# A table of 187 numbers that moves tasks in the priorities of a list schedule

## The chip, the cores and the metric

One core of one Trainium2 chip. The core has five instruction queues: PE (TensorE, matrix products), DVE (VectorE), ACT (ScalarE), POOL (GpSimd) and SP (SyncE, which here only starts DMA transfers). Each runs its own instructions in the order in which they were written, and waits on semaphores for the others. The metric is the device time of one execution, in microseconds.

## The reference

```
# q, k, v: 8 x 8 x 576 x 64, phi: 8 x 8 x 576 x 32 (batch, heads, tokens, ...)
a = softmax(phi, axis=2)                           # over the 576 tokens
k_m = einsum('bhsm,bhsd->bhmd', a, k)              # 32 memories per head
v_m = einsum('bhsm,bhsd->bhmd', a, v)
attn = softmax(q @ k_m.T / sqrt(64), axis=-1)
x = (attn @ v_m), heads side by side               # 4608 x 512
h = x @ w_in                                       # w_in: 512 x 2048
out = maximum(h, 0)**2 @ w_out                     # w_out: 2048 x 512
```

The two weights come as 64-bit floats.

## The kernel before

**The numerics.** Products run on PE in `fp32r`, and an operand that has to be more exact is kept as a high and a low part, so that a product becomes three matmuls (high by high, high by low, low by high). `decode` turns each 512 KB piece of 64-bit weights into such a pair with a chain of DVE and ACT instructions (L417 to L437, and L450 for the last subtraction). Where the weight goes into `wo`, the low part of the later pieces is added by a DMA that POOL issues (L454).

**The work.** A batch of 576 tokens is one step, and its heads are handled in two halves (`u` is batch and half, as `5_0`). `memory` loads `phi`, `k` and `v`, takes the maximum over the tokens (L516 on DVE, then two transposes on PE, L518 and L521), and forms `k_m` and `v_m` (L540, into the PSUM tile `pkv`). `vw_step` and its relatives multiply `v_m` into `w_in`, so that attention times that product (`vw`) gives `h` without forming `x` (tiles `pvw`, `vw`). `scores`, `first_attention` and `attention` give the softmax `S`, its transpose (`pat`, `at`) and the pair `ath`, `atl`. `mm1` forms `h` (L923), and `r`, `gh`, `glo` are its relu, its square and the low part of the square. `mm2` adds the product with `wo` into `acc` (L953, L954, L956). From the 96th of these steps `fast` does the same with seven products in place of eight for each pair of 256-wide pieces (its `H`, `M` tiles, L1086 and L1115).

**Buffers.** A buffer name stands for a slot that is used again and again, and whoever writes next waits for all that used it before. Two are of interest. The slot `mx` holds both the maximum of L516 and, for batches 5 to 7, the transposed memories `kT`, which POOL stores to DRAM at L601 (`kT_kept`):

```
        mx = st([P, P], F32, "mx", f"mx{u}")
        kT = st([P, 2, 1, M], F32, f"kT{b % 2}{hh}" if b <= QUAD else "mx", f"kT{u}")
```

The weights `wi` that SyncE loads again for the later batches (L461) rotate through three slots, each of which comes free when PE has used the piece in it (L670).

**The order.** None of this is issued as it is written. Each operation is first recorded by `Plan.op`, with the engines that may run it and a cost on each (`ways`), and with what it depends on. `Plan.order` then makes list schedules. Each operation gets a key from how late it may be, `forward` plays the five engines and the wire with these costs and always takes, on an engine that is free, the ready operation of the smallest key, and several rounds with other keys (`backward`) are tried. The keys of the best round are played once more, and the operations are written in the order of the start times that this gives. Where an operation may run on two engines, the play also settles which one.

## Time and profile before

| | |
|---|---|
| median of 3 runs | 770.11 us (768.22 to 772.91) |
| the profiled execution | 768.92 us |
| its span, first to last instruction | 767.2 us |
| mean granted TensorE clock | 0.994 of full speed |
| PE busy | 740.4 us, 97% of the span |
| DVE, ACT, POOL busy | 605.3, 411.1, 75.9 us (79%, 54%, 10%) |

The profiled execution is 1.7 us longer than its span; that part lies before the first and after the last instruction. PE's busy time counts overlapping matmuls once. What PE waits for is read from the list of its waits, and where it waits from the instructions in order of time.

### The profile page before, as it was taken

The numbers are of one execution on the slowest core, as the hardware profiler recorded it, in microseconds if no ns is written. First come the engines' busy times: TensorE is split into PE (matmuls) and PEld (weight loads), VectorE is DVE, ScalarE is ACT, GpSimd is POOL, SyncE is SP. The second block draws the span as 40 slices with busy tenths as digits, with TensorE's granted clock in tenths as the row PEclk, the third lists the DMA queues.
The fourth block names the chain that finished last, engine by engine and source line by source line (L and its number), as shares of the span: only waits on it lengthen the run. The fifth ranks groups of instructions, "written<-read, shape, count | busy, mean of one in ns | idle before, by whom it ended". The sixth has DMA issues, their size and how long they took to land.

```text
span 767.2 us, 14774 instructions
## 1 busy us (share of the span) xinstructions
PE 740.4 (97%) x5374; PEld 649.5 (85%) x5374; DVE 605.3 (79%) x1405; ACT 411.1 (54%) x933; POOL 75.9 (10%) x133
## 2 busy tenths in 40 slices
PE   5988999999999999999999999999999999999997
PEld 3767898888888887888888788888888899999997
DVE  4899999997669798776659445579999868996875
ACT  2666788775653554534345234345565735666642
POOL 4101211110100000001010221111000100000000
PEclk9989999999999999999999999999999999999999
DMA  8987987478755946554385877875410345445421
GB/s 266 321 283 193 290 243 240 166 209 237 210 137 147 275 117 175 176 164 116 102 299 168 276 216 260 269 230 114 109 37 1 73 121 156 138 114 174 129 82 42
DMA packets 82632, 135.62 MB, mean 177 GB/s; under 512 B 26080, under 2 KB 52704, under 8 KB 82560
## 3 DMA queue, kind: packets, MB, share of 16 engines
q1 hardware_dynamic: 67168, 98.40, 44.2%
q0 software_dynamic: 15296, 36.15, 15.7%
q8 instruction: 43, 0.70, 0.4%
q14 instruction: 29, 0.24, 0.1%
q10 hardware_dynamic: 96, 0.13, 0.1%
HBM read 96.14 MB, written 34.80 MB: 171 GB/s over the span
## 4 chain that ended last, share of the span: by engine, by line
PE 44%; issue 33%; DVE 9%; DMA 7%; POOL 4%; ACT 1%; SPq 1%; POOLq 0%; DVEq 0%; ACTq 0%
PE h L1058 7%; PE h L923 6%; PE acc L956 4%; PE acc L953 4%; PE acc L954 4%; POOL vw_kept L709 2%; DMA out_dram<-o 2%; PE accl L1169 2%; DMA wo<-work 2%; PE pkv L540 2%; PE accl L1184 1%; DMA raw<-in_moe_w_out_dram 1%; PE pvw L670 1%; PE psc L753 1%; PE Mb L1115 1%
## 5 line engine op out<-in xcount | busy, mean ns | idle before, releaser
L923 PE MATMUL h<-ath,vw 128*128 128x320 f32 (+1 forms) x768 | 159.2, 301 | 1.4 <-ACT ath L846 0.9
L953 PE MATMUL acc<-wo,gh 128*128 128x512 f32 x384 | 156.6, 408 | 0.4 <-ACT gh L929 0.4
L954 PE MATMUL acc<-wo,gh 128*128 128x512 f32 x384 | 151.1, 393 | 1.4 <-DMA wo<-work 1.4
L923 PEld LDWEIGHTS h<-ath,vw 128*128 128x128 f32 x768 | 127.0, 190 | 12.4 <-ACT r L927 1.6
L956 PE MATMUL acc<-wo,glo 128*128 128x512 f32 x384 | 117.3, 402 | 0.8 <-DVE glo L933 0.7
L927 ACT ACTIVATE r<-h 128x256 f32<-128x256 f32 (+1 forms) x142 | 57.1, 408 | 61.8 <-PE h L923 56.3
L929 ACT ACTIVATE gh<-r 128x512 fp32r<-128x512 f32 x96 | 60.7, 632 | 47.9 <-DVE r L928 39.1
L953 PEld LDWEIGHTS acc<-wo,gh 128*128 128x128 f32 x384 | 72.3, 188 | 15.6 <-ACT gh L929 0.9
L954 PEld LDWEIGHTS acc<-wo,gh 128*128 128x128 f32 x384 | 72.4, 188 | 14.3 <-DMA wo<-work 1.7
L923 PE MATMUL h<-atl,vw 128*128 128x320 f32 (+1 forms) x384 | 82.9, 297 | 0.5 <-DVE atl L847 0.5
L956 PEld LDWEIGHTS acc<-wo,glo 128*128 128x128 f32 x384 | 68.9, 189 | 13.8 <-DVE glo L933 1.4
L933 DVE TENSOR_TENSOR glo<-r,gh 128x512 fp32r<-128x512 f32 x96 | 65.3, 681 | 5.5 <-ACT r L931 4.6
L923 PEld LDWEIGHTS h<-atl,vw 128*128 128x128 f32 x384 | 62.2, 190 | 0.8 <-DVE atl L847 0.8
L1058 PE MATMUL h<-ath,vw 128*128 128x256 f32 (+1 forms) x256 | 52.3, 296 | 0.0
L345 ACT CAST vw<-pvw 64x512 fp32r<-64x512 f32 (+1 forms) x64 | 37.1, 580 | 22.7 <-PE pvw L670 19.5
L931 ACT ACTIVATE r<-r 128x576 f32<-128x576 f32 x68 | 46.6, 685 | 1.6
L928 DVE TENSOR_SCALAR r<-h 128x320 f32<-128x320 f32 (+1 forms) x50 | 22.8, 457 | 25.5 <-PE h L923 25.1
L1058 PEld LDWEIGHTS h<-ath,vw 128*128 128x128 f32 x256 | 39.9, 188 | 0.5 <-issue 0.2
L678 DVE TENSOR_TENSOR vw<-pvw,vw 64x512 fp32r<-64x512 f32 x48 | 33.0, 686 | 2.0 <-ACT vw L345 1.0
L932 DVE TENSOR_TENSOR r<-r 128x576 f32<-128x576 f32 x28 | 21.2, 757 | 15.6 <-ACT gl L930 13.6
L709 POOL DMA_DIRECT2D vw_kept<-fold x32 | 17.3, 540 | 111.3 <-DVE fold L706 91.5
L753 PE MATMUL psc<-qT,kb 128*128 128x256 f32 (+1 forms) x96 | 27.5, 408 | 0.2 <-DVE S L757 0.2
(251 smaller groups left out, 1615.1 us busy)
## 6 DMA issues: line engine op xcount, KB each, us to landing
vw<-vw_kept SPq DMA_DIRECT2D x192, 128.0 KB, 3.1
wi<-w_in_kept SPq DMA_DIRECT2D x40, 512.0 KB, 5.0
vw_kept<-fold POOLq DMA_DIRECT2D x32, 512.0 KB, 4.2
KV<-in_k_dram SPq DMA_DIRECT2D x16, 512.0 KB, 4.3
KV<-in_v_dram SPq DMA_DIRECT2D x16, 512.0 KB, 5.5
raw<-in_moe_w_out_dram SPq DMA_DIRECT2D x16, 512.0 KB
raw<-in_moe_w_in_dram SPq DMA_DIRECT2D x16, 512.0 KB, 4.8
w_in_kept<-wi POOLq DMA_DIRECT2D x16, 512.0 KB, 5.2
```

The source lines that it names most:

```text
L345: nc.scalar.copy(o, i) if e == "ACT" else ENG[e].tensor_copy(o, i)
L678: vec({"DVE": 700}, lambda e, part=part, pr=pr: nc.vector.tensor_sub(part(1), pw()[pr], part(0).bitcast(F32)), [pw, (V, (0, hf))], [(V, (1 ...
L753: nc.tensor.matmul(pq()[:, 0:32 * n], kb()[:, x].rearrange("p h m -> p (h m)"), qT()[:, x, 0:n].rearrange("p c t -> p (c t)"), start=(x == ...
L923: nc.tensor.matmul(p()[:, 0:n], V()[:, l, hh, c0:c0 + P], x()[:, hh, cs], start=(i == 0), stop=(i == 5))
L927: op({"ACT": act(n) - 40, **({} if b < 2 else {"DVE": tt(n)})}, lambda e, cs=cs, n=n, p=p: nc.scalar.activation(r()[:, cs], p()[:, 0:n], A ...
L929: op({"ACT": act(SM)}, lambda e: nc.scalar.activation(gh(), r()[:, 0:SM], AF.Square), [r], [gh])
L931: op({"ACT": act(S), **({} if b < 2 or b == FAST - 1 else {"DVE": tt(S)})}, lambda e: nc.scalar.activation(r(), r(), AF.Square) if e == "A ...
L933: vec({"DVE": tt(SM)}, lambda e: nc.vector.tensor_sub(glo(), r()[:, 0:SM], gh().bitcast(F32)), [r, gh], [glo])
L953: nc.tensor.matmul(a(), gh()[:, c], t()[:, 0], start=f0, stop=False)
L954: nc.tensor.matmul(a(), gh()[:, c], t()[:, 1], start=False, stop=False)
L956: nc.tensor.matmul(a(), glo()[:, c], t()[:, 0], start=False, stop=f1)
L1058: nc.tensor.matmul(p()[:, at:at + n], V()[:, l, hh, f0:f0 + P], x()[:, hh, cs], start=(i == 0), stop=(i == 5))
```

## The change

Each call of a function that is marked `plan.named` begins a new task, each call's end another, and so does every twelfth operation within one; tasks are numbered in the order of recording, up to about 1000. `MOVED` gives 187 of them a number. After the best keys are found, each operation of task n has its key changed by 100 times `MOVED[n]`, in the unit of the keys (ns), and the last play of `forward` uses these keys. Nothing else differs: operations, buffers, transfers and their sizes are the same. Since the new text stands above the rest, a line n of the kernel before is some 20 to 60 lines further down in the changed one (L518 has become L562, L923 L975, L953 L1006).

```
+PART = 12
+MOVED = {
+    10: 23, 11: 291, 12: 70, 16: 47, 18: 49, 22: -30, 26: -2, 30: -23, 32: 201, 34: 36, 36: 18, 40: 85, 42: 47,
...
+    979: -46, 989: -18, 990: 35, 995: 320,}
...
+    def begin(self):
+
+        self.tasks += 1
+        self.task, self.steps = self.tasks, 0
+
+    def named(self, fn):
+
+        def run(*args, **more):
+            self.begin()
+            got = fn(*args, **more)
+            self.begin()
+            return got
+
+        return run
...
+        if self.steps == PART:
+            self.begin()
+        self.steps += 1
...
+        o.task = self.task
...
-        self.forward(best[1])
+        moved = [k + 100 * MOVED.get(o.task, 0) for k, o in zip(best[1], self.ops)]
+        self.forward(moved)
...
+    @plan.named
     def decode(kind, j, h, room):
...
+    @plan.named
     def memory(b, hh, where=None):
```

The same mark stands on `wi_again`, `vw_alone`, `vw_step`, `vw_quad`, `vw_again`, `scores`, `first_attention`, `attention`, `mm1`, `mm2`, `combine`, `fast` and `fast_left`.

**What moves in the start-up.** PE's queue around the second transposes of the first attention (`pat0_1`, from the softmax `S0_1`), before:

```order
L540 MATMUL pkv1_0_495<-KV1_0_273,phi1_0_215 32x64 x40
L843 MATMUL pat0_1_591<-ident_63,S0_1_436 128x128 x4
L850 MATMUL patl0_599<-ident_63,S0_1_436 128x128
L923 MATMUL h0_0_614<-ath0_474,vw0_0_0_454 128x256 x2
L923 MATMUL h0_0_614<-atl0_536,vw0_0_0_454 128x256 x2
L923 MATMUL h0_0_614<-ath0_474,vw0_0_0_454 128x256 x2
L651 MATMUL pvw0_1_0_626<-wi0_1_0_597,VTh00_89 128x256 x4
L651 MATMUL pvw0_1_0_626<-wi0_1_0_597,VTl00_95 128x256 x2
L576 MATMUL pkt1_0_636<-ident_63,kvx1_0_623 128x128
L923 MATMUL h0_1_640<-ath0_474,vw0_0_0_454 128x320 x2
```

and after:

```order
L584 MATMUL pkv1_0_496<-KV1_0_278,phi1_0_215 32x64 x40
L620 MATMUL pkt1_0_603<-ident_63,kvx1_0_589 128x128
L620 MATMUL pvt1_0_610<-ident_63,kvx1_0_589 128x128
L893 MATMUL pat0_1_615<-ident_63,S0_1_431 128x128 x4
L900 MATMUL patl0_622<-ident_63,S0_1_431 128x128
L696 MATMUL pvw0_1_0_624<-wi0_1_0_596,VTh00_89 128x256 x4
L696 MATMUL pvw0_1_0_624<-wi0_1_0_596,VTl00_95 128x256 x2
L696 MATMUL pvw0_1_0_624<-wi0_1_1_559,VTh00_89 128x256 x4
L696 MATMUL pvw0_1_0_624<-wi0_1_1_559,VTl00_95 128x256 x2
L562 MATMUL pmx1_1_645<-ident_63,mx1_1_599 128x128
L975 MATMUL h0_0_648<-ath0_474,vw0_0_0_472 128x256 x2
```

The transposes `pkt1_0` and `pvt1_0` of batch 1's memories and the twelve `pvw0_1_0` matmuls, which stood behind the first group of `h`, now stand ahead of it, and so does `pmx1_1`.

DVE's queue at the same place, up to the last multiplication of that softmax (L867), before:

```order
L865 TENSOR_SCALAR rz0_1_526<-rz0_1_526 128x20
L847 TENSOR_TENSOR atl0_536<-pat0_0_464,ath0_474 128x512
L421 TENSOR_SCALAR work_518<-work_518 128x512
L866 RECIPROCAL rz0_1_526<-rz0_1_526 128x20
L435 SCALAR_TENSOR_TENSOR work_518<-raw_380,work_518 128x512
L867 TENSOR_TENSOR S0_1_436<-S0_1_436,rz0_1_526 128x640
L437 TENSOR_TENSOR work_518<-work_518 128x512
L437 TENSOR_TENSOR work_423<-work_423 128x512
```

and after (the multiplication is L917):

```order
L479 TENSOR_TENSOR work_436<-work_436 128x512
L463 TENSOR_SCALAR work_519<-work_519 128x512
L914 TENSOR_REDUCE rz0_1_581<-S0_1_431 128x20
L477 SCALAR_TENSOR_TENSOR work_519<-raw_380,work_519 128x512
L622 SCALAR_TENSOR_TENSOR kvx1_0_589<-pkv1_0_496,rs1_0_526,par_76 128x128
L479 TENSOR_TENSOR work_519<-work_519 128x512
L915 TENSOR_SCALAR rz0_1_581<-rz0_1_581 128x20
L621 TENSOR_SCALAR kvx1_0_589<-pkv1_0_496,rs1_0_526 128x128
L916 RECIPROCAL rz0_1_581<-rz0_1_581 128x20
L560 TENSOR_REDUCE mx1_1_599<-phi1_1_309 128x128
L917 TENSOR_TENSOR S0_1_431<-S0_1_431,rz0_1_581 128x640
```

Five instructions, the two L437 of `decode`, two for `kvx1_0` and the maximum `mx1_1`, and the small reciprocal of `rs1_0`, have passed from behind it to ahead of it.

**What moves near 284 us.** PE's queue, with the product `pvw1_4_0` that frees a slot of `wi`, and `pkv5_0`, the memories of half 5_0, before:

```order
L555 MATMUL pkv5_0_3440<-ones_70,asum5_0_3420 128x1
L953 MATMUL acc2_0_1_3187<-wo20_935,gh36_3411 128x512
L954 MATMUL acc2_0_1_3187<-wo20_935,gh36_3411 128x512
L670 MATMUL pvw1_4_0_3449<-wi1_4_0_3250,VTh10_2284 128x256 x2
L670 MATMUL pvw1_4_0_3449<-wi1_4_0_3250,VTl10_2298 128x256
L670 MATMUL pvw1_4_0_3449<-wi1_4_0_3250,VTh10_2284 128x256 x2
L670 MATMUL pvw1_4_0_3449<-wi1_4_0_3250,VTl10_2298 128x256
L540 MATMUL pkv5_0_3440<-KV5_0_3131,phi5_0_2990 32x128 x20
```

and after, the product, and then `pkv5_0` with its neighbours (18 rows lie between the two):

```order
L716 MATMUL pvw1_4_0_3443<-wi1_4_0_3216,VTh10_2296 128x256 x2
L716 MATMUL pvw1_4_0_3443<-wi1_4_0_3216,VTl10_2304 128x256
L716 MATMUL pvw1_4_0_3443<-wi1_4_0_3216,VTh10_2296 128x256 x2
L716 MATMUL pvw1_4_0_3443<-wi1_4_0_3216,VTl10_2304 128x256
L975 MATMUL h38_1_3454<-ath2_2836,vw1_0_3_3308 128x320 x2
L975 MATMUL h38_1_3454<-atl2_2845,vw1_0_3_3308 128x320 x2
```

```order
L1006 MATMUL acc2_0_0_3123<-wo21_959,gh37_3485 128x512
L1007 MATMUL acc2_0_0_3123<-wo21_959,gh37_3485 128x512
L584 MATMUL pkv5_0_3494<-KV5_0_3179,phi5_0_3007 32x128 x20
L1009 MATMUL acc2_0_1_3186<-wo20_954,glo36_3388 128x512
L1006 MATMUL acc2_0_1_3186<-wo21_959,gh37_3485 128x512
```

The product has moved from right ahead of `pkv5_0` to well ahead of it; the maximum `pmx5_1`, 32 rows behind `pkv5_0` in both, is still that far behind. The slot of `wi` that the product frees is the one for `wi1_5_1`, which SyncE loads next.

**What moves near 605 us.** ACT's queue at the first step of `fast`, with the two casts of `H96`, before:

```order
L345 COPY o5_2_6974<-acc5_0_2_6212 128x512
L1076 ACTIVATE XD_6960<-XD_6960 128x256
L345 COPY o5_1_6985<-acc5_0_1_6204 128x512
L1002 CAST wo71_2070<-E7_1_6902 128x256
L345 COPY o5_3_6999<-acc5_0_3_6219 128x512
L1086 CAST H96_7002<-X96_6950 128x512
L1086 CAST H96_7002<-XD_6960 128x384
```

and after:

```order
L1117 ACTIVATE XD_6952<-h96_0_6927 128x256
L1131 ACTIVATE XD_6952<-XD_6952 128x256
L386 COPY o5_0_6975<-acc5_0_0_6187 128x512
L1056 CAST wo71_2094<-E7_1_6925 128x256
L1141 CAST H96_6991<-X96_6942 128x512
L386 COPY o5_3_7002<-acc5_0_3_6255 128x512
L1117 ACTIVATE X97_7008<-h97_0_6979 128x256
L1141 CAST H96_6991<-XD_6952 128x384
```

Of the four copies `o5_x`, three stood ahead of the casts here and one was on DVE; now one stands ahead of them, one between them, and two are on DVE. On PE, the six matmuls of `h97_0` that stood behind the first products `Mb96` now stand ahead of them.

## Rows read from the trace of the kernel before

**Rows 1.** The page: the span, the busy time of each engine, and the chain of work that ended last by engine.

```profile
span 767.2 us, 14774 instructions
...
PE 740.4 (97%) x5374; PEld 649.5 (85%) x5374; DVE 605.3 (79%) x1405; ACT 411.1 (54%) x933; POOL 75.9 (10%) x133
...
PE 44%; issue 33%; DVE 9%; DMA 7%; POOL 4%; ACT 1%; SPq 1%; POOLq 0%; DVEq 0%; ACTq 0%
```

**Rows 2.** Busy time by stretch of the span, whole program. Columns: stretch and its length, busy us (instructions) of PE, PEld, DVE, ACT and POOL, the granted TensorE clock as a share of full speed, the share of DMA, GB/s.

```profile
44.60:51.50 6.90, 5.55 (x23) 5.20 (x23) 6.02 (x14) 3.50 (x10) 1.06 (x2) 0.51 1.06 329
...
60.00:200.00 140.00, 137.37 (x981) 118.88 (x980) 129.01 (x270) 104.17 (x226) 23.32 (x33) 1.00 0.77 226
200.00:760.00 560.00, 556.66 (x3849) 494.11 (x3848) 430.37 (x1033) 276.77 (x645) 39.36 (x72) 1.00 0.53 154
```

**Rows 3.** Waits of PE: the instruction and what it waited for, us in total, times, longest.

```profile
PE pat L843 <- DVE S L867: 1.7, 1, 1.7
...
PE pmx L518 <- DVE mx L516: 1.5, 1, 1.5
...
PE acc L954 <- DMA wo<-work: 1.4, 1, 1.4
PE Mb L1115 <- ACT H L1086: 1.1, 1, 1.1
```

**Rows 4.** PE between 40 and 60 us in order of time. Columns: start us, us, engine, line, operation, out<-in, shape, count, [idle before it <- what ended that].

```profile
43.77 0.66 PE L843 MATMUL pat<-ident,S 128*128 128x128 f32 x4 [1.71 <-DVE S L867]
...
45.51 0.58 PE L923 MATMUL h<-ath,vw 128*128 128x256 f32 x1 [0.85 <-ACT ath L846]
...
46.81 0.58 PE L923 MATMUL h<-atl,vw 128*128 128x256 f32 x1 [0.50 <-DVE atl L847]
...
58.90 0.30 PE L518 MATMUL pmx<-ident,mx 128*128 128x128 f32 x1 [1.59 <-DVE VTl L629]
59.41 0.73 PE L956 MATMUL acc<-wo,glo 128*128 128x512 f32 x2 [0.21 <-DVE glo L933]
```

**Rows 5.** DVE in the same stretch, the same columns.

```profile
43.64 1.29 DVE L437 TENSOR_TENSOR work<-work 128x512 f32<-128x512 f32 x2
44.84 0.15 DVE L569 RECIPROCAL rs<-rs 128x1 f32<-128x1 f32 x1
44.91 1.24 DVE L516 TENSOR_REDUCE mx<-phi 128x128 f32<-128x640 f32 x1
...
47.47 0.34 DVE L578 SCALAR_TENSOR_TENSOR kvx<-pkv,rs,par 128x128 f32<-128x128 f32 x1
47.73 0.34 DVE L577 TENSOR_SCALAR kvx<-pkv,rs 128x128 f32<-128x128 f32 x1
```

**Rows 6.** The second half of `wo20` on DVE and POOL, then its use on PE, the same columns.

```profile
73.12 0.68 DVE L450 TENSOR_TENSOR wo<-work,wo 128x512 fp32r<-128x512 f32 x1
...
74.10 0.88 POOL L454 DMA_DIRECT2D wo<-work  x1 [1.58 <-DVE wo L450]
...
81.24 0.50 PE L953 MATMUL acc<-wo,gh 128*128 128x512 f32 x1 [0.39 <-ACT gh L929]
83.13 0.50 PE L954 MATMUL acc<-wo,gh 128*128 128x512 f32 x1 [1.38 <-DMA wo<-work]
```

**Rows 7.** The DMAs that POOL issues at L454 between 70 and 90 us, from issue to landing.

```profile
DMA to landing us min/median/max: 5.2/8.7/9.0
```

**Rows 8.** The store of `kT5_0` near 287 us. First SyncE's queue and POOL, then the time to landing of this store and of the three stores after it, then DVE and PE; columns as in rows 4.

```profile
284.31 0.32 SPq L461 DMA_DIRECT2D wi<-w_in_kept  x1
285.71 0.38 SPq L470 DMA_DIRECT2D KV<-in_k_dram  x1
...
301.48 0.32 SPq L461 DMA_DIRECT2D wi<-w_in_kept  x1
304.49 0.38 SPq L470 DMA_DIRECT2D KV<-in_k_dram  x1
...
287.14 0.57 POOL L601 DMA_DIRECT2D kT_kept<-kT  x1 [1.20 <-DVE vx L604]
...
DMA to landing us min/median/max: 6.3/6.3/6.3
...
DMA to landing us min/median/max: 3.6/3.7/3.9
...
293.48 1.25 DVE L516 TENSOR_REDUCE mx<-phi 128x128 f32<-128x640 f32 x1 [1.46 <-DMA kT_kept<-kT]
...
284.00 0.28 PE L670 MATMUL pvw<-wi,VTl 128*128 128x256 f32 x1
...
294.88 0.30 PE L518 MATMUL pmx<-ident,mx 128*128 128x128 f32 x1 [1.47 <-DVE mx L516]
```

**Rows 9.** The start of the last stage near 605 us: ACT, then PE, the same columns.

```profile
605.65 0.41 ACT L1002 CAST wo<-E 128x256 fp32r<-128x256 f32 x1
605.96 0.59 ACT L345 COPY o<-acc 128x512 f32<-128x512 f32 x1
606.44 0.63 ACT L1086 CAST H<-X 128x512 fp32r<-128x512 f32 x1
...
607.12 0.39 PE L1115 MATMUL Mb<-wo,H 128*128 128x256 f32 x1 [1.11 <-ACT H L1086]
```

18 lines of the change are left out of this document (17 added, 1 removed), and 15 rows, old and new, of the table MOVED.

## The prediction

> **What bounds the kernel now.** I read the page first [rows 1]: PE is busy for 740.4 us of a span of 767.2, every other engine far less, and the chain that ended last is PE's own time and the time in which PE's instructions merely follow one another ("issue"). So the end moves only if PE's matmuls change or if PE waits more or less. The change leaves the matmuls as they are, and the question is what happens to the 27 us in which PE is idle. The busy time by stretch [rows 2] says where they are: 2.6 us between 60 and 200 us (140.00 less 137.37), 3.3 us between 200 and 760, and so about 21 us in the first 60 us and behind 760. What lies ahead of the first matmul and behind the last one has no earlier work to take its place, and I count it as fixed. The list of PE's waits [rows 3] then names the few that can be had singly: 1.7 us for the softmax `S0_1`, 1.5 for the maximum of a later batch, 1.4 for the DMA that completes `wo20`, 1.1 for `H96` at the start of the last stage. An instruction that moves elsewhere in the program changes nothing unless it touches one of these or makes a new one. The start-up has one more property: in 44.6 to 51.5 us the granted clock is 0.51, the lower of its two levels (1.2 GHz), and full on both sides of it [rows 2].
>
> **The change part by part.** Each operation keeps its cost, so only waits are priced, and the sum is made against the profiled execution of 768.92 us (span 767.2, and 1.7 around it), which is 1.2 us under the median of 770.11.
>
> *Squarings.* Eleven squarings of `r` pass from DVE to ACT, and a dozen other instructions change engine, in both directions. Both engines are below 80% of the span [rows 1]: 0.
>
> *The start-up.* On DVE five instructions now stand ahead of the last multiplication of `S0_1`. By their rows [rows 5] they last 1.29 (two of L437), 1.24, 0.34 and 0.34 us, with the 0.15 of the small reciprocal 3.36 in all; neighbours overlap at their ends, so I take 3.0. `pat0_1`, which starts at 43.77 as soon as that multiplication is done [rows 4], would start 3.0 us later, and with it everything that PE has queued behind it, the first `h` above all. What comes back: behind `pat0_1` PE waits 0.85 for `ath`, 0.50 for `atl`, 1.59 for the low part of `VT` ahead of `pmx1_1`, and 0.21 for `glo0` [rows 4], together 3.15 us. In the new order the twelve `pvw0_1_0` matmuls stand where PE waits for `ath` and `atl`, the memories of batch 1 are turned before `pat0_1` and not after, and `glo0` comes earlier on DVE. I take all four as gone. By 60 us the two nearly cancel (3.0 less 3.15).
>
> Whatever is left over then meets a gate. The second term of `acc0_0_0` with `wo20` needs the low part that POOL's DMA adds. DVE finishes it at 73.80, POOL issues the DMA at 74.10, and PE can go on at 83.13 [rows 6], about 9.0 us after the issue; of three such DMAs the median takes 8.7 [rows 7]. PE stood ready 1.38 us earlier, after 0.39 for `gh` [rows 6]. In the order the same amount of matmuls lies ahead of this one before and after, and on DVE the same instructions lie ahead of the L450 that feeds it, but for a few casts and subtractions of 64 columns that make up 0.2 us. So an earlier PE waits longer at the gate, a later one (by up to 1.38 + 0.39 = 1.77 us) less, and the gate moves only with DVE. I take -0.3. The ends: if none of the 3.15 comes back and the lower clock lasts as much longer as `pat0_1` is later, 3.36 + 1.68 - 1.77 = +3.3; if this DMA landed in 5.2 us like the quickest of the three [rows 7], 5.2 - 9.0 = -3.8.
>
> The page DMA: Bandwidth & Descriptors of the Trainium skill (section Anatomy of one DMA — SWDGE (gpsimd) path) gives for a DMA issued by POOL about 2.0 us plus the bytes at 436 GB/s. For 256 KB that would be an estimate of 2.6 us. The trace differs, with 5.2 to 9.0 us [rows 7], and by the page's figure the gate would be open before PE comes.
>
> *Near 293 us.* PE waits 1.47 us for the maximum of `phi` (`mx5_1`), and DVE, which forms it, has itself waited 1.46 for a DMA, the store of `kT5_0` whose slot it overwrites [rows 8]. The store is issued at 287.14 and lands 6.3 us later, where the three stores after it take 3.6 to 3.9 [rows 8]. Around all of them the loads of `k`, `v` and `phi` run. What is special at the first is a 512 KB load of `wi` issued at 284.31, 1.4 us ahead of them; at the second store that load is 3.0 us ahead (301.48 against 304.49) [rows 8]. The load of 284.31 was held by the product `pvw1_4_0`, whose last matmul starts at 284.00 [rows 8] directly ahead of `pkv5_0`. With the change this product stands 19 rows earlier, some 4 us by the 0.2 to 0.3 us of such a row, and the load goes out that much before the others. I expect the store to land in 3.9 us, 2.4 earlier. PE's work between `pkv5_0` and `pmx5_1` is about as long as before (32 rows in both), so 1.4 of the 1.47 us goes. That SyncE now loads `phi6_0` ahead of `KV5_1` there does nothing, since both wait for the same release. What DVE does between is next in line: ten rows of its queue stand between `kT5_0` and `mx5_1`, and I judge that they end with the store. Ends: -1.5 and +0.3.
>
> *Near 605 us.* ACT casts `H96` at 606.44 behind a copy of 0.59 and a cast of 0.41, and PE waits 1.11 us for it [rows 9]. Two copies fewer now stand ahead of the cast on ACT (2 x 0.59 = 1.18), and the six matmuls of `h97_0` stand on PE where it waited. Against that, one of the copies is now on DVE ahead of the sums that `H96` is made from. I take -0.8, and -1.1 to 0 as the ends.
>
> *Elsewhere.* Of the 6.0 us that PE is idle between 60 and 760 us, 1.77, 1.47 and 1.11 are the waits above. The rest, 1.6 us, is small waits that an order with other neighbours may lose or make. In the new order several `glo` and relus stand closer ahead of the matmuls that read them. I take +0.4, with -1.0 and +3.0 (about twice the rest) as the ends.
>
> Sum: 0 - 0.3 - 1.4 - 0.8 + 0.4 = -2.1 us, 766.8 for the execution and, from the median of 770.11, 768.0.
>
> **The rivals.**
>
> The gate opens early (faster). If the accumulating DMA lands in 5.2 us, for which the spread of the three landings speaks, and against which two of the three speak [rows 7], the start-up gives -3.8: -3.8 - 1.4 - 0.8 + 0.4 = -5.6, 764.5. It decides only if PE is at the gate by then, which needs the 3.15 us to have come back. Chance 0.12. The Trainium skill's figure for such a DMA, above, is on the side of this rival.
>
> The stores of `kT` (slower). All halves from 5_0 on put `kT` into the slot of the next maximum. If the new order brings the `wi` loads close ahead of the others at the four halves from 5_0 to 6_1, each costs what the one did, 1.5 us, and in place of -1.4 there is +6.0 - 1.5 = +4.5. With the other terms +3.8, 773.9; with the upper end of the start-up as well +7.4, 777.5. The point from which it decides is a landing of about 4.8 us (6.3 less 1.5), and three of four stores keep 0.9 us from it now [rows 8]. Chance 0.13.
>
> Nothing moves (770.1). The start-up's delay and returns cancel, DVE is late for `mx5_1` and for `H96`, and all waits are only renamed. For it speaks that PE is at 97% [rows 1] and that only 4.4 us of idle time lie in named waits behind 60 us. Chance 0.20.
>
> The forecast itself has the remaining 0.55.
>
> **How the numbers follow.** A measurement of this kernel tells about 1% (7.7 us) from no change. Faster by that needs less than 762.4: all favourable ends together, -3.8 - 1.5 - 1.1 - 1.0 = -7.4, only just reach it. I give 0.11, most of it for a start-up that gains more than I see. Slower by that means over 777.8, which the second rival reaches with the upper end of the start-up, or the small waits in quantity: 0.12. Within 1%: 0.77. The range goes from the favourable ends, 762.5, to 774.5 (the second rival and a little more), and leaves out about 2 in 10.
>
> **What would show each step.** In the profile after: `pat0_1` at about 46.8 us with a wait of 3 to 5 us for S; no wait for `ath`, `atl` and `VTl` behind it; a wait of PE for the DMA into `wo` near 82 us, of 1.4 to 3 us, ended at 82.5 to 83; no wait of PE for `mx` over 0.3 us between 280 and 300, and a store of `kT` that lands in under 4.5 us; a wait for `H96` under 0.4 us. Busy time of PE within 2 us of 740. The prediction is wrong if the gate near 83 is gone or comes later than 84, if PE shows new waits of over 1 us behind 100 us, or if the lower clock lasts beyond 56 us.

## Result and profile after

The changed kernel takes 774.43 us (median of 20 runs, 768.88 to 784.75), the kernel before 769.25 beside it (20 runs, 762.89 to 774.71): a ratio of 1.0063 [1.0043, 1.0082], 0.6% or about 4.8 us slower. The forecast was 768.0, 2.1 us faster, and the slow end of its range was 774.5.

The page after, in the lines that answer to [rows 1]; the profiled execution took 774.48 us:

```profile
span 772.8 us, 14817 instructions
PE 742.2 (96%) x5374; PEld 652.3 (84%) x5374; DVE 600.5 (78%) x1396; ACT 416.8 (54%) x942; POOL 74.9 (10%) x133
PE 67%; issue 15%; DMA 7%; DVE 4%; POOL 2%; SPq 1%; ACT 1%; POOLq 0%; DVEq 0%; ACTq 0%
```

PE's busy time is 1.8 us longer with the same 5374 matmuls, the span 5.6. So most of the loss is PE's waiting, and PE's waits after, beside [rows 3], say where it is new:

```profile
PE acc L1009 <- DVE glo L985: 3.0, 2, 2.1
PE acc L1007 <- DMA wo<-work: 2.9, 1, 2.9
PE pkt L620 <- DVE kvx L621: 2.8, 1, 2.8
PE h L1113 <- DMA vw<-vw_kept: 1.7, 2, 1.0
PE acc L1006 <- ACT gh L981: 1.0, 1, 1.0
```

Of the four single waits of [rows 3], those for `mx` (near 293 us) and `H96` are gone, the one for `S` has become one for `kvx`, and the one for the DMA into `wo` has doubled. The waits for `glo` and `gh` have grown (0.7 and 0.4 us before), and the one for `vw` is new. The longest wait of either list, for the first `pmx` at 6 us, has hardly changed (5.9 and 6.2).

The start-up in order of time, on PE, then POOL, ACT, DVE (columns as in [rows 4]), and two stretches with the columns of [rows 2]:

```profile
46.37 0.30 PE L620 MATMUL pkt<-ident,kvx 128*128 128x128 f32 x1 [2.76 <-DVE kvx L621]
...
48.26 1.12 PE L893 MATMUL pat<-ident,S 128*128 128x128 f32 x4 [0.44 <-DVE S L917]
...
84.22 0.50 PE L1007 MATMUL acc<-wo,gh 128*128 128x512 f32 x1 [2.94 <-DMA wo<-work]
...
107.07 0.96 PE L1009 MATMUL acc<-wo,glo 128*128 128x512 f32 x3 [2.11 <-DVE glo L985]
...
75.44 0.89 POOL L496 DMA_DIRECT2D wo<-work  x1 [3.32 <-DVE VTl L673]
...
87.63 0.59 ACT L843 COPY qT<-pq 128x512 f32<-128x512 f32 x1 [4.47 <-PE pq L840]
...
88.78 0.69 DVE L462 SCALAR_TENSOR_TENSOR work<-work 128x512 uint32<-128x512 uint32 x1 [2.49 <-ACT work L460]
...
105.26 0.43 DVE L459 TENSOR_SCALAR work<-raw 128x512 f32<-128x512 f32 x1 [2.88 <-DMA wo<-work]
...
47.00:54.20 7.20, 6.41 (x29) 6.12 (x30) 5.70 (x14) 3.00 (x10) 1.06 (x2) 0.53 1.10 335
...
84.50:88.20 3.70, 3.70 (x15) 3.34 (x15) 1.79 (x5) 0.57 (x2) 0.00 (x0) 0.54 0.91 318
```

They can be read as one chain. PE stands 2.94 us at the gate, the term of `acc0_0_0` with `wo20`. In the 3.7 us behind it the granted clock is 0.54, about the lower level, in a stretch that [rows 2] have at full clock. The `pq` matmuls stand behind the gate in PE's queue, and ACT's copy of their result waits 4.47 us for them. Behind that copy ACT has the step of the next expert's decode, for which DVE waits 2.49. So the low part of `wo31` reaches POOL late, and the slot of `work` that its DMA reads stays in use: DVE waits 2.88 us to write there, and the `glo` that stands two instructions behind on DVE holds PE for 2.11 us at 107 us. The rows show each wait; that each follows from the one before is an argument, and the experiments below test it.

Near 469 us, ACT, then PE:

```profile
469.38 0.59 ACT L386 CAST fold<-pvq_pa 128x512 fp32r<-128x512 f32 x1 [7.04 <-DMA vw_kept<-fold]
469.86 0.63 ACT L981 ACTIVATE gh<-r 128x512 fp32r<-128x512 f32 x1
...
470.55 0.50 PE L1006 MATMUL acc<-wo,gh 128*128 128x512 f32 x1 [0.99 <-ACT gh L981]
...
472.20 0.73 PE L1009 MATMUL acc<-wo,glo 128*128 128x512 f32 x2 [0.92 <-DVE glo L985]
```

This is the same pattern: ACT's cast waits for a store that POOL issued, and the `gh` for which PE waits stands behind the cast.

To compare whole executions I looked up where PE starts the matmul that has the same amount of matmul work ahead of it, and took the difference to the profiled execution of before: the **lag**, in us. Its steps show where a kernel loses or gains. The columns are the amount of work, in us; 28 lies near 57 us of the span, 46 just ahead of the gate, 150 behind the start-up, 250 behind 293 us of the span, 400 to 410 around 469 us, 540 behind 605 us. In gate_warm its 24 added transposes are not counted as work.

```
kernel           28    46   150   250   400   410   540   719
after           2.8  -0.6   5.0   2.6   4.4   6.8   3.3   5.9
start_old       1.5   1.5   0.1  -2.9  -1.0   4.9   1.3   4.8
start_new       2.0  -1.4   7.7   6.0   6.0   6.0   7.6   7.9
end_new         3.5   3.5   2.9   1.9   1.8   1.8   2.5   7.1
late_new       -2.3  -2.2  -3.1  -3.5  -3.3  -3.3  -4.9  -4.4
gate_warm      -1.5  -4.7  -1.3  -4.0  -2.2  -1.3  -4.8  -1.3
gate_dve_old    1.7   2.3   1.7   1.3   1.2   1.2   1.2   0.8
gate_dve_new    1.5  -1.8   1.0  -2.2  -0.4   3.7   0.2   5.4
four_dve_new    2.4  -1.0   1.2  -2.2  -0.4   2.9  -0.6   4.0
four_dve_old    1.3   3.6   5.2   7.0   7.7   7.7   7.5   7.5
both_mended     2.2  -1.0   0.3  -3.0  -1.2   2.3  -1.1   2.2
start_old_fold  2.4   2.4   2.6  -0.9   1.0   2.2  -1.4   3.4
```

The column 28 differs by up to 6 us between executions whatever the order (below), so steps are compared, not ends. Each row is one execution; where two kernels share a stretch of instructions, their steps there differ by up to 3.5 us (start_new and after from 46 to 150).

### The profile page after: what moved, and what is told of

The parts are those of the page before. It is cut to its first block, busy times and chain, and to the rows that moved or that the text cites. A ratio compares the mean times of both kernels' runs of the same rounds, so it can differ in the third digit from the quotient of the medians.

```text
span 772.8 us, 14817 instructions
## 1 busy us (share of the span) xinstructions
PE 742.2 (96%) x5374; PEld 652.3 (84%) x5374; DVE 600.5 (78%) x1396; ACT 416.8 (54%) x942; POOL 74.9 (10%) x133
## 4 chain that ended last, share of the span: by engine, by line
PE 67%; issue 15%; DMA 7%; DVE 4%; POOL 2%; SPq 1%; ACT 1%; POOLq 0%; DVEq 0%; ACTq 0%
PE h L975 14%; PE acc L1006 8%; PE acc L1009 8%; PE acc L1007 8%; PE h L1113 6%; PE accl L1225 3%; PE psc L802 2%; PE pvw L716 2%; DMA wo<-work 2%; DMA vw_kept<-fold 2%; PE pkv L584 2%; PE accl L1241 1%; DMA vw<-vw_kept 1%; POOL vw_kept L756 1%; PE pvw L696 1%
## 5 line engine op out<-in xcount | busy, mean ns | idle before, releaser
L975 PE MATMUL h<-ath,vw 128*128 128x256 f32 (+1 forms) x768 | 158.2, 302 | 0.0
L1006 PE MATMUL acc<-wo,gh 128*128 128x512 f32 x384 | 156.0, 406 | 1.1 <-ACT gh L981 1.0
L975 PEld LDWEIGHTS h<-ath,vw 128*128 128x128 f32 x768 | 125.4, 189 | 10.5 <-ACT r L979 1.0
L1009 PE MATMUL acc<-wo,glo 128*128 128x512 f32 x384 | 127.5, 403 | 3.0 <-DVE glo L985 3.0
L979 ACT ACTIVATE r<-h 128x320 f32<-128x320 f32 (+1 forms) x145 | 58.3, 409 | 59.2 <-PE h L975 52.4
L1006 PEld LDWEIGHTS acc<-wo,gh 128*128 128x128 f32 x384 | 72.5, 189 | 15.8 <-ACT gh L981 1.4
L975 PE MATMUL h<-atl,vw 128*128 128x256 f32 (+1 forms) x384 | 82.4, 296 | 0.0
L975 PEld LDWEIGHTS h<-atl,vw 128*128 128x128 f32 x384 | 62.0, 190 | 0.0
L1113 PE MATMUL h<-ath,vw 128*128 128x256 f32 (+1 forms) x256 | 53.0, 298 | 2.1 <-DMA vw<-vw_kept 1.7
L983 ACT ACTIVATE r<-r 128x576 f32<-128x576 f32 x79 | 54.1, 685 | 1.6
L980 DVE TENSOR_SCALAR r<-h 128x256 f32<-128x256 f32 (+1 forms) x47 | 21.3, 453 | 18.3 <-PE h L975 17.6
L1113 PE MATMUL h<-atl,vw 128*128 128x320 f32 (+1 forms) x128 | 27.3, 294 | 0.0
```

The lines of the kernel that those rows point to most:

```text
L975: nc.tensor.matmul(p()[:, 0:n], V()[:, l, hh, c0:c0 + P], x()[:, hh, cs], start=(i == 0), stop=(i == 5))
L979: op({"ACT": act(n) - 40, **({} if b < 2 else {"DVE": tt(n)})}, lambda e, cs=cs, n=n, p=p: nc.scalar.activation(r()[:, cs], p()[:, 0:n], A ...
L983: op({"ACT": act(S), **({} if b < 2 or b == FAST - 1 else {"DVE": tt(S)})}, lambda e: nc.scalar.activation(r(), r(), AF.Square) if e == "A ...
L1006: nc.tensor.matmul(a(), gh()[:, c], t()[:, 0], start=f0, stop=False)
L1009: nc.tensor.matmul(a(), glo()[:, c], t()[:, 0], start=False, stop=f1)
L1113: nc.tensor.matmul(p()[:, at:at + n], V()[:, l, hh, f0:f0 + P], x()[:, hh, cs], start=(i == 0), stop=(i == 5))
```

## Experiments

### Which stage loses

Six kernels take the instructions from the old order up to a point of the planner's time and from the new one behind it, or the reverse. The edit is the same in all:

```
-        self.forward(moved)
-        out = sorted(self.ops, key=lambda o: (o.start, o.seq))
+        plans = {}
+        for name, k in (("old", best[1]), ("new", moved)):
+            self.forward(k)
+            plans[name] = [(o, o.start, o.left) for o in sorted(self.ops, key=lambda o: (o.start, o.seq))]
+        out, done = [], set()
+        for name, until in SEGMENTS:
+            for o, start, left in plans[name]:
+                if start < until and o.seq not in done:
+                    o.left = left
+                    done.add(o.seq)
+                    out.append(o)
```

**The start from the old order, the rest new.** `+SEGMENTS = ("old", 129000), ("new", 1000000000),`

> The order of before up to about 135 us of the execution, the changed order from there on. Theory 1, the loss is made in the start-up: up to 110 us the changed kernel has fallen 5.2 us behind at equal matmul work, and all of that is kept to the end; then this kernel takes about 769 us, the 5.2 us less than the changed one, with no wait of PE near 107 us and the wait for the DMA into wo at 83 us as short as before (1.4 us). Theory 2, the loss is made behind 135 us (new waits near 470 and from 640 to 720 us, 2.4 and 2.5 us), and a start-up that is behind gets its time back at waits that come later: then it takes 773 to 775 us, like the changed kernel.

0.9994 [0.9962, 1.0025]: not slower. Without the new start the total shows no loss. The trace shows something else too, a step of +5.9 between 400 and 410, where ACT's cast of `fold` waits 7.95 us; it is made up between 150 and 250 and from 410 to 540.

**The start from the new order, the rest old.** `+SEGMENTS = ("new", 123000), ("old", 1000000000),`

> The changed order up to about 135 us, the order of before from there on, the counterpart of the kernel above. Theory 1: it falls 5 us behind by 110 us and stays there, about 774 us, with the wait at 84 us, the lower clock behind it, and the wait for glo near 107 us. Theory 2: the order of before behind 135 us takes the delay back, 769 to 771 us.

1.0045 [1.0021, 1.0069]. The new start alone loses most of what the whole loses. PE waits 3.35 us at the gate, the lag steps from -1.4 to 7.7 and then stays between 6.0 and 7.9. The step is larger than after (5.6), and in this execution the granted clock falls a second time, behind a wait of 1.86 us for `glo` at 106 us, as the first row shows. The second row is the wait for `H96`, which the order behind the joint still has, as in [rows 9]:

```profile
107.80:111.20 3.40, 3.40 (x14) 3.01 (x14) 3.40 (x9) 1.56 (x4) 0.00 (x0) 0.51 0.50 153
...
614.76 0.39 PE L1180 MATMUL Mb<-wo,H 128*128 128x256 f32 x1 [1.11 <-ACT H L1151]
```

**The middle alone.** `+SEGMENTS = ("old", 207000), ("new", 330000), ("old", 474000), ("new", 603000), ("old", 1000000000),`

> The order of before, but the changed order in two stretches, 215 to 345 and 490 to 628 us. In the changed kernel PE gains 2.4 us on the kernel before in the first and 3.3 in the second. If these gains belong to the order of the stretch itself (theory 1), this kernel takes 5 to 6 us less than before, about 763.5 us, without the wait for mx near 293 us and without that for H96 near 607. If they are only time that the changed kernel, being late, takes back from waits for DMAs that were due anyway (theory 2), PE gains less than 2 us in the two together.

1.0031 [1.0013, 1.0050]. Each joint left a wait of its own (1.13, 1.53, 0.93 and 1.00 us), so this kernel tells little. It shows the gain at `H96` (-1.4 between 500 and 540) without the rest.

**The end alone.** `+SEGMENTS = ("old", 613000), ("new", 1000000000),`

> The order of before up to about 630 us, the changed order behind it. Theory 1: the new waits for vw there (0.6 and 1.0 us) and for a copy (0.4) belong to the order of the last stage and cost 2.5 us: about 771.7 us. Theory 2: they come from a DMA queue that is late from before, and with the earlier order of before ahead of them they are absent: 769 to 770 us.

1.0038 [1.0011, 1.0065]. The new order loses behind 640 us as well: the lag steps by 4.6 from 540 on, where kernels with the old order there (start_new, gate_dve_old, late_new) step by -0.4 to 0.5. The waits of PE show the loads of `vw`:

```profile
PE h L1123 <- DMA vw<-vw_kept: 3.6, 4, 1.2
```

**The stretch that gains, alone.** `+SEGMENTS = ("old", 474000), ("new", 603000), ("old", 1000000000),` for late_new, and 410000 and 590000 in the place of 474000 and 603000 for late_new2.

> The order of before, but the changed order from about 490 to 628 us. Theory 1 (the changed order is better there by itself): PE gains 2 to 3 us on the kernel before by 615 us, the wait for H96 near 607 us goes, and of this 2 us stay to the end: about 768.5 us where before takes 770.5. Theory 2 (what it gains there it had lost near 470 us, where the same work was moved, or the joint at 628 us gives it back): within 1 us of before.

> The same with other joints, 425 and 615 us, so that the changed order's waits near 470 us (1.0 and 0.9 us) are inside. Theory 1 (these waits are the price of the gain that follows): PE loses 2 us or more near 470 us, gains 3 us until 610 us, and ends 1 to 2 us ahead of before. Theory 2 (the waits near 470 us come from being late there): no wait over 0.5 us near 470 us, and 3 us gained.

1.0008 [0.9975, 1.0040] and 1.0069 [1.0041, 1.0097]. The stretch around 605 us gains (-1.6 between 410 and 540 in late_new), but a joint costs as much (PE waits 1.43 and 2.18 us at it). None of the parts tried makes the old order faster.

### Is it the five instructions ahead of S0_1?

Six kernels move a few operations, with all that depends on them, behind another one of the list, everything else in its order. The edit behind the sort, for all of them:

```
+        for late, anchor in DEFERRED:
+            at = next(i for i, o in enumerate(out) if o.seq == anchor)
+            held, head = set(), []
+            for o in out[:at + 1]:
+                if o.seq in late or any(d.seq in held for d in o.deps):
+                    held.add(o.seq)
+                    head.append(o)
+            assert anchor not in held
+            out = [o for o in out[:at + 1] if o.seq not in held] + head + out[at + 1:]
```

**The five DVE instructions back behind the multiplication of `S0_1`.** `+DEFERRED = [((187, 198, 441, 442, 443, 457), 89)]`

> The changed order, but the last multiplication of S0_1 stands again ahead of the two L437 of decode, the two kvx1_0 products, the maximum mx1_1 and a small reciprocal on DVE (in fact ahead of five of the six, as one L437 stands before them all). Theory 1 (that these five make DVE late for wo20): pat0_1 starts about 2 us earlier, DVE finishes wo20 at about 73.8 us as before, the gate opens 1 us earlier, and PE is 2 us or more earlier at 100 us than in the changed kernel. Theory 2 (DVE's time of that L450 is set by its own work, which is the same, and by its waits ahead of 40 us): the gate opens as late as in the changed kernel, within 0.5 us.

1.0038 [1.0010, 1.0066]. PE waits 4.06 us for `kvx` in the place of 2.76, and 2.42 at the gate, which opens at 84.35: theory 2, by the gate. The interval overlaps that of the change. Putting back what the prediction followed step by step does not take the loss away.

### Is it the gate?

**The old order, with DVE held up ahead of `wo20`** by four copies of a half of `work` onto itself. `+EXTRA = 4`

```
-            vec({"DVE": tt(ND)}, lambda e: nc.vector.tensor_sub(part(1), wf(), part(0).bitcast(F32)),
-                [wk, k0], [k1], lead=True)
+            def last(e):
+                for _ in range(EXTRA if late and (j, h) == (2, 0) else 0):
+                    nc.vector.tensor_copy(tf(), tf())
+                nc.vector.tensor_sub(part(1), wf(), part(0).bitcast(F32))
+
+            vec({"DVE": tt(ND)}, last, [wk, k0], [k1], lead=True)
```

> The order of before, with four more copies in place on DVE (128x512) ahead of the L450 that completes the high part of wo20, so that the DMA behind it lands later by their time, some 1.4 to 2.4 us. Theory 1 (a long gap at the gate costs more than itself): PE's wait for that DMA near 83 us grows from 1.4 to about 3 us, the granted clock then falls to its lower level for 3 to 4 us as behind the changed kernel's gap of 2.9 us, and PE is 3 us or more behind the kernel before at 100 us, 1.4 us more than the copies take. Theory 2 (the gap costs itself): PE is behind by the time of the copies and no more, and the clock stays full behind 80 us.

1.0016 [0.9990, 1.0042], and neither theory as written: PE did not get to the gate first, since it stood ahead of it for a `glo` that DVE had late. The granted clock was then at its lower level for 6.8 us:

```profile
78.94 1.65 PE L1024 MATMUL acc<-wo,glo 128*128 128x512 f32 x3 [2.18 <-DVE glo L1000]
...
78.30:85.10 6.80, 6.17 (x23) 5.68 (x24) 5.21 (x13) 1.97 (x5) 1.46 (x2) 0.50 0.94 238
```

The lag steps by +4.6 from 28 to 46 (2.1 to 6.7), more than the 1.73 us by which this wait is longer than in the kernel before (0.45), and by -1.4 from there to 150, since PE finds the gate open. So a gap cost more than itself here too, though not at the gate and not clear of noise in the total.

**The new order, with matmuls that need no `wo20` put ahead of the gate**: `pvw0_3_0`, `pq`, `pql` and `psc`. `+DEFERRED = [((317, 318, 319, 320), 495)]`

> The changed order, but on PE four pieces of work that don't need wo20 (the first matmuls of pvw0_3_0, the transposes pq1_1_1 and pql1, and one of the score products) are put ahead of the first product with wo20, 3.2 us of matmuls. Theory 1: the wait for the DMA at 84 us falls from 2.9 to under 1 us, the clock stays full behind it, and PE is 3 to 4 us earlier at 100 us than in the changed kernel, so about 770.5 us. Theory 2 (something else holds PE there, as the decode chain on DVE): PE waits as long at the next products with wo, and less than 1.5 us is gained by 110 us.

1.0083 [1.0057, 1.0108], worse. The wait at the gate is gone, and PE waits for `wi`, `qT`, `qx` and `glo` instead (0.53 to 1.26 us each): ACT and DVE are no further than PE there. The granted clock fell all the same, against theory 1, and for longer than after:

```profile
82.40:92.60 10.20, 8.46 (x33) 7.11 (x32) 8.78 (x20) 3.97 (x8) 1.90 (x3) 0.50 0.95 295
```

So this kernel does not tell what the wait at the gate alone costs.

**The new order, with 24 transposes that nobody reads in the gap at the gate**, so that PE does not idle there. `+EXTRA = 24`

```
+                    if (g, i, l) == (4, 0, 0):
+                        for _ in range(EXTRA):
+                            nc.tensor.transpose(PW[3, 0]()[:, 0:P], ident, ident)
```

> The changed order, and PE turns a constant 24 times (128x128, about 0.11 us each at full clock, 2.6 us) into a bank that is free, ahead of the first product with wo20, where it would stand idle for 2.9 us; nothing else uses that. Theory 1 (part of the loss is the lower clock behind the idle): the gate opens at the same time, the clock stays full between 80 and 100 us, and PE is 1.3 us less behind at 90 us. Theory 2 (the clock doesn't follow from the idle there, or costs nothing since DVE and ACT are the limit): the same lag as the changed kernel at 100 us, within 0.5 us.

1.0036 [1.0007, 1.0065], an interval that overlaps that of the change. This execution is some 4 us ahead of after as a whole, so its gate opens at 79.71, 8.4 us after the issue, and not at 84.22. The transposes fill the wait, and behind the gate the clock is full, with 22 matmuls in 3.5 us where after has 15 in 3.7. The wait for `glo` is there as before:

```profile
76.76 2.78 PE L1019 MATMUL pvw<-ident 128*128 128x128 f32 x24
...
79.71 0.50 PE L1022 MATMUL acc<-wo,gh 128*128 128x512 f32 x1
...
79.70:83.20 3.50, 3.50 (x22) 3.10 (x22) 2.65 (x7) 1.34 (x3) 0.00 (x0) 1.00 0.99 338
...
100.90 0.98 PE L1024 MATMUL acc<-wo,glo 128*128 128x512 f32 x3 [2.03 <-DVE glo L997]
```

The order on PE is otherwise that of after, so the two can be compared matmul by matmul: gate_warm is 4.1 us earlier ahead of the gate and 6.1 to 6.3 us earlier from 50 to 150 us of work. So the lag steps by 3.4 from 46 to 150, not 5.6. Theory 1 holds in the trace: the full clock gave back about 2 us of the step (0.4 of them because the DMA landed a little sooner), and the wait for `glo` did not take it.

**The new order, with the DVE instruction that waits for the slot of `work` (L459) moved behind the `glo`.** `+DEFERRED = [((700,), 396)]`

> The changed order, but one DVE instruction, the first of a decode (L417 of the kernel before) that overwrites a work slot which the DMA of wo31 still reads, is put three rows later, behind the glo for which PE waits 2.1 us near 107 us. Theory 1: that wait goes and with it 2 us to the end, about 772.4 us. Theory 2: PE then waits for the next result of the same decode, and less than 1 us is gained by 120 us.

**The new order, with ACT's copy of `pq` moved behind the decode step that it holds.** `+DEFERRED = [((492,), 361)]`

> The changed order, but on ACT one copy (the third quarter of qT1, which needs a transpose that stands behind the gate on PE) is put behind the next step of the decode of wo30 and the cast of wi0_3_1, so that these two no longer wait for the gate. Theory 1 (the stall goes on through the queues: PE's gate holds ACT for 4.5 us, ACT holds DVE for 2.5, the DMA of wo31 is late by that, and so is the work slot for which DVE and then PE wait near 105 us): DVE's wait of 2.5 us near 88 us goes, the DMA of wo31 is issued about 2 us earlier, and the wait near 107 us falls from 2.1 to under 0.7 us, about 772.5 us. Theory 2 (the wait near 107 us has another cause): it stays over 1.5 us.

1.0048 [1.0019, 1.0077] and 1.0092 [1.0064, 1.0120]. In the first the wait near 107 us goes to an instruction of ACT, in the second DVE waits longer than before:

```profile
107.08 0.74 PE L706 MATMUL pvw<-wi,VTh 128*128 128x256 f32 x4 [1.80 <-ACT vw L396]
```

```profile
91.42 0.69 DVE L502 TENSOR_TENSOR wo<-work,wo 128x512 fp32r<-128x512 f32 x1 [3.44 <-ACT wo L396]
```

In both, the granted clock was at its lower level again (0.50 over 81.8 to 88.2, and 84.8 to 88.2). Neither edit took out the link that it was meant for without making another wait, so the chain behind the gate is not shown link by link.

**The gate taken away.** DVE adds the low part of `wo20` where POOL's DMA did, in the new order and in the old one (there `self.forward(best[1])` plays the keys that are not moved). `+ON_DVE = ((2, 0),)`

```
-            dma(lambda d: d(out=part(1), in_=tf(), accum_op=ALU.add), ...
+            def add(d):
+                if (j, h) in ON_DVE:
+                    nc.vector.tensor_add(part(1), part(1).bitcast(F32), tf())
+                else:
+                    d(out=part(1), in_=tf(), accum_op=ALU.add)
+
+            dma(add, ...
```

> The new order throughout; the low part of wo20 is added to it by DVE (one instruction of 512 columns, some 0.68 us, in the place where POOL issued the DMA) and not by POOL's DMA. So the gate of acc0_0_0 opens with DVE, some 7 us earlier than PE comes. Theory 1 (the idle time at the gate, the lower clock behind it and what ACT, DVE and the next DMA lose by it are the loss of the start-up): no wait of PE over 0.5 us between 80 and 86 us, granted clock 1.00 from 56 to 120, ACT's wait of 4.5 us for pq gone, and a time 3 to 5 us below the new order's, ratio 0.999 to 1.002. Theory 2 (the decode on DVE and ACT is what PE waits for in the new start, the gate only its first sign): PE waits 2 us or more for glo, wi or qT between 80 and 110 us all the same, ratio 1.004 to 1.008.

> The old order throughout, with the same edit for wo20. It is the counterpart: in the old order PE waits 0.9 to 1.5 us at the gate and the clock stays full. Both theories: the wait for the DMA into wo near 82 us goes; DVE has 0.68 us more to do ahead of the next glo, so 0.997 to 1.001. Where the new order with this edit is not slower than this kernel, the new start is not worse in itself but only meets the gate.

1.0059 [1.0026, 1.0092] and 1.0019 [0.9986, 1.0052]. By the total, theory 1 fails. By the trace of the start it holds in part: the wait for `wo20` is gone, the clock is full from 56 to 120 us, and the step from 46 to 150 is 2.8 and not 5.6. But PE now waits 1.02 us for the next DMA of POOL, that of `wo21`, and still for `qT` (1.26) and `glo` (1.40), which is theory 2's part:

```profile
85.88 0.50 PE L1014 MATMUL acc<-wo,gh 128*128 128x512 f32 x1 [1.02 <-DMA wo<-work]
```

In this execution PE then lost 4.1 us where the order has its next place of this kind, between 400 and 410, and 5.2 from 540 on:

```profile
465.87 0.50 PE L1013 MATMUL acc<-wo,gh 128*128 128x512 f32 x1 [1.15 <-ACT gh L988]
...
467.53 1.22 PE L1016 MATMUL acc<-wo,glo 128*128 128x512 f32 x2 [0.92 <-DVE glo L992]
...
460.00:475.00 15.00, 12.93 (x66) 10.38 (x65) 5.71 (x11) 3.38 (x8) 1.17 (x2) 0.89 0.70 218
```

**All four of `wo20`, `wo21`, `wo30` and `wo31` on DVE**, `+ON_DVE = ((2, 0), (2, 1), (3, 0), (3, 1))`, in either order.

> The new order; the low parts of wo20, wo21, wo30 and wo31 all added by DVE (4 x 0.68 = 2.7 us more on DVE, four DMAs less on POOL). With it goes what held DVE for 2.88 us at 102.4 us, a slot of work that the late DMA of wo31 still read. Theory 1: no wait of PE for glo near 107 us, 0.996 to 1.001. Theory 2: DVE, the limit of the start, has 2.7 us more, PE's waits for glo between 80 and 120 us grow to 3 us or more in all, 1.005 to 1.010.

> The old order with the same four additions on DVE. Theory 1: the gate's wait goes and no other comes, 0.996 to 1.001. Theory 2: as in the kernel with four copies ahead of wo20 (2.7 us of work on DVE, about 2 us lost), 1.002 to 1.004.

1.0040 [1.0003, 1.0076] and 1.0053 [1.0022, 1.0083]. The new order's start now steps by 2.2 from 46 to 150, and PE waits for no `glo` and for no DMA into `wo` in it (1.99 us for `qT` remain); that the further additions on DVE cost anything does not show. In the old order the lag steps by 2.3 ahead of 46 and by 1.6 behind it, but there the clock fell at a place where it is full in the kernel before, so what the additions cost in it is not shown:

```profile
62.10:65.50 3.40, 3.40 (x10) 2.66 (x9) 3.40 (x6) 2.29 (x5) 0.56 (x1) 0.50 0.98 246
```

With `wo20` on DVE the new start is not the worse of the two: from 28 to 150 the lag steps by -0.5 in gate_dve_new and by -1.2 in four_dve_new, by 0.0 in gate_dve_old. With the DMAs it is: by +2.2 in after and +5.7 in start_new, against -1.4, -0.6, -0.8 and +0.2 in start_old, end_new, late_new and start_old_fold. Of the kernels of the table with the new start and the DMAs only gate_warm, at full clock, is as low (+0.2).

### The second place, near 466 us

**ACT's cast of `fold` moved behind the two `gh` that stand behind it**, `+DEFERRED = [((2461,), 2472)]`, with the new order and `wo20` on DVE, and with the start of the old order.

> The new order with two edits: wo20's low part added by DVE as in gate_dve_new, and, near 469 us, ACT's cast of fold (with DVE's subtraction and POOL's store that hang on it) moved behind the two gh that stand behind it. In the new order this cast waits 7.04 us for the store of the fold before, and PE then waits 0.99 for gh and 0.92 for glo; with the gate gone PE came earlier and waited 1.15 and 0.92 there at a clock that fell, 4.2 us lost in all. Theory 1 (what the new order loses is lost where a queue is held by an instruction that waits for a DMA issued by POOL, and a gain ahead of such a place is given back there until it is mended too): no wait of PE over 0.5 us and full clock between 460 and 480, a lead kept through there, 3 to 4 us less than gate_dve_new, ratio 1.000 to 1.002. Theory 2 (the stages behind are limited by the transfers themselves, and PE only meets them elsewhere): the lag behind the kernel before that gate_dve_new has at the end, some 5 us, comes back by other waits, ratio 1.004 to 1.007.

> The old order up to about 135 us and the new one behind it, as in start_old (0.9994), with the same move of the cast of fold near 465 us. There the cast waited 7.95 us for the store ahead of it, PE 1.91 and 0.73, the granted clock fell to 0.77 of full in that stretch and 5.9 us were lost. Theory 1: these go, ratio 0.993 to 0.997, faster than both kernels. Theory 2: another wait takes them back, 0.998 to 1.001.

1.0009 [0.9981, 1.0037] and 1.0001 [0.9973, 1.0028]. With both places edited the new order is no slower than the kernel before; its interval lies below that of the change. No version beats the kernel before. But with the old start the move changes nothing in the total (0.9994 without it), and in the traces it is no clear gain: the step from 400 to 410 is 1.2 in start_old_fold (5.9 without the move), but 3.5 in both_mended (4.1 without it, 2.4 after). In both kernels the second cast of the pair now waits for the same stores, 3.69 and 3.99 us, and PE behind it 1.22 and 2.07. In both_mended:

```profile
469.54 0.58 ACT L397 CAST fold<-pvq_pv 128x512 fp32r<-128x512 f32 x1 [3.99 <-DMA vw_kept<-fold]
...
470.95 0.35 PE L763 MATMUL pvq_pv<-wi,VTh 64*128 64x256 f32 x1 [2.07 <-issue]
```

The profile names no releaser for PE here; that it waited for the buffer `pvq_pv`, which this cast reads, is inferred from the names. What both_mended gains on after in these executions lies in the start, which steps by 1.3 from 46 to 150 (2.8 in gate_dve_new with the same start). So the total shows that the two edits together take the loss away, not what the second one adds.

## Why the prediction was wrong

**The step that failed** is the one that an earlier PE merely "waits longer at the gate" and that "the gate moves only with DVE", and with it the -0.3 for the start-up. (By the prediction's own terms it would have been 0: 3.0 less 3.15 is a lead of 0.15, which the gate takes.) PE was earlier: 3.4 us by the lag from 28 to 46. In this stretch PE idled for 2.4 of 23 us before, and hardly at all after:

```profile
57.00:80.00 23.00, 20.64 (x223) 16.83 (x222) 22.07 (x52) 14.51 (x33) 4.87 (x7) 1.00 0.75 204
...
59.30:79.00 19.70, 19.69 (x221) 16.64 (x220) 19.27 (x44) 14.55 (x33) 4.83 (x7) 1.00 0.83 230
```

The delay of `pat0_1`, priced at 3.0, cost about 1 us ahead of that (the lag is 1.6 at 22 us of work and 2.8 at 28): PE waited 2.76, 0.68 and 0.44 us there in place of 1.71, 0.85 and 0.50. PE did wait longer at the gate, 2.94 for 1.38 [rows 6]. But a longer wait is not free. The step from 46 to 150 is +5.6, where the lead of 3.4 alone would have been used up, so the start ends 2.2 us behind in this execution (5.7 in start_new, by the same reckoning). What takes the rest is what the prediction never asked of the gap. One part is the clock: at full clock the step is 3.4 (gate_warm). The other is what is queued behind the waiting matmul on PE and who waits for that, up to the 2.11 us for `glo` at 107. The gate opened at 84.22, just past the 84 that I had named as the sign of an error, and 8.8 us after the issue (9.0 before): DVE's part of it was 1.3 us later than in the profile of before (74.46 against 73.12 [rows 6]), where I had 0.2. With the old start it opens at 84.12 in start_old, so this shift belongs to the execution; there PE comes 2 us later than after and waits 0.86.

That 774.43 still lies inside the range is luck: the slow end came from the stores of `kT`, none of which made a wait.

**The signs named ahead.** `pat0_1` came at 48.26 and not at 46.8; the wait of 3 to 5 us showed in three pieces, 2.76 for `kvx`, then 0.68 and 0.44. The waits for `ath`, `atl` and `VTl` are gone, as said. PE's busy time, 742.2, is just outside 2 us of 740. Two signs for "wrong" came true besides the gate's time: new waits of over 1 us behind 100 us, at 107 and 720, and the lower clock, which returned behind the gate, well beyond 56 us.

**Near 293 us.** No wait for `mx` after, as forecast, but the -1.4 was no property of the order. Of seven other executions with the old order there, six show no such wait over 0.4 us (the seventh, four_dve_old, has 1.88). I priced a wait of one execution as if it stood in all.

**Near 605 us.** Right: the wait for `H96` recurs wherever the old order stands there (1.11 in start_new, end_new and three more) and is gone with the new one; its share of the lag is -1.3 to -1.4, forecast -0.8 (its favourable end was -1.1).

**Elsewhere** was the second mis-sized term: +0.4, with ends of -1.0 and +3.0. After, the lag steps by +4.2 between 250 and 410, by -3.5 from there to 540 and by +2.6 from 540 on. Three terms of several us that nearly cancel were called "small waits". The last is no accident of one execution: all seven other kernels of the table with the new order at the end step by 3.3 to 5.2 there, and the four with the old one by -0.4 to 0.5. In the trace of before PE is busy for 40.00 of the 40 us from 440 and for 80.00 of the 80 from 640, so nothing there had a row to price; the ACT cast that waits 7.04 us at 469 was to be found only by asking which instructions in the new queue wait for a store of POOL, and what now stands behind them.

**The rivals.** The gate did not open early: the three DMAs landed in

```profile
DMA to landing us min/median/max: 3.3/8.7/9.4
```

of which that of `wo20` took the 8.7; in [rows 7] it was the slowest, with 9.0. The Trainium skill's formula for a DMA issued by POOL (page DMA: Bandwidth & Descriptors, section Anatomy of one DMA — SWDGE (gpsimd) path), an estimate of 2.6 us, is not borne out by this trace either. No store of `kT` made a wait, so the slower side came by another mechanism than the rival named for it. All favourable ends together, -7.4, give 762.7, which does not reach the 762.4 that the prediction compares them with.

**Shown and not shown.** Shown by totals: that the new start loses (start_new slower, start_old not), that the new end loses by itself (end_new), and that with `wo20` on DVE and the cast of `fold` moved the loss is no longer measurable (1.0009). Shown by the traces of single executions: that the DMA of `wo20` makes half or more of the start's step (2.8 and 1.3 without it, 5.6 with it), some 2 us of that by the clock (gate_warm), and that PE loses time near 466 us in every kernel of the table with the new order there, 0.9 to 5.9 us, and in none with the old one (act_first, which is not in the table, loses nothing there). Argued only: the chain behind the gate link by link, that a lead gained at the start is what is lost near 466 us, and that the order of SyncE's loads of `vw` makes the loss at the end (in the kernels of the table PE waits for these loads there, up to 1.7 us at a time). Open: why start_old, which has the new end, shows no loss in the total, and which of the two edits of both_mended brings its gain. The total of gate_dve_new alone does not differ from that of the change.

## What to carry to other kernels

A wait for an event at a fixed time does not simply absorb an earlier arrival: list what is queued behind the waiting instruction, who waits for that, and whether the engine's clock holds, before the gap is costed at nothing. In a list schedule look for every instruction that waits for a slow DMA with an operand of the busiest engine behind it in the same queue; mending one such place may not show in the total (gate_dve_new, 1.0059) while others are left. A wait that one profiled execution shows is a term of the sum only where other executions show it too.

## What the runs showed of the hardware

The granted clock was 0.54 over the 3.7 us behind PE's wait of 2.94 us at 84 us, with PE busy all the time. How long PE waits does not tell by itself whether it falls. After waits of 1.15 and 0.92 us, with 0.7 us of matmuls between them, it was 0.89 over 460 to 475 in gate_dve_new. With waits of 1.91 and 0.93 there it stayed at 1.00 in four_dve_new, and with 1.91 and 0.73 it was 0.77 in start_old; the lag steps by 3.3 in the first and 5.9 in the second. The old start, whose waits of 0.39 and about 1 us at the gate leave the clock full in the kernel before, met the lower level behind them in start_old_fold (0.50 over 85.4 to 88.8).

Executions that share the old start differ by up to 5.8 us at 28 us of work (end_new 3.5, late_new -2.3). The 16 matmuls of the first scores, in the kernel before and in late_new:

```profile
22.17 3.65 PE L814 MATMUL psc<-kbd,qT 128*128 128x64 f32 x16 [0.48 <-ACT qT L793]
```

```profile
22.26 1.97 PE L874 MATMUL psc<-kbd,qT 128*128 128x64 f32 x16 [0.67 <-ACT qT L853]
```

The same work at the same time takes 3.65 or 1.97 us, though the views print a granted clock of 1.00 in both. The `pd` matmuls behind it take 2.02 or 1.08. The traces account for it: their list of granted levels has its first entry, full clock, at 27.6 us in the kernel before and at 21.4 in late_new, and where the list has no entry a view prints 1.00. Ahead of the first entry the rows run at about half speed. All the profiled executions but before have that entry between 29.2 and 31.5 us, except late_new and gate_warm (21.3), the two with a lag below zero at 28; both took some 5 us less than their kernel's median (764.51 for 769.72, 767.34 for 772.55). So the start of the full clock makes a part of the spread of 12 us between the runs of one kernel (762.89 to 774.71 before), and a single profile can hide or feign a change of this size.
